# One more Strassen round of the first MoE layer in each of the last two chunks, with part of the side work on GpSimd

## The chip, the cores and the metric

The kernel runs on one core of one Trainium2 chip. The metric is the device time of one execution in microseconds (us); the median of the runs shown is compared.

## The reference

The reference is an attention with "beacon" keys, followed by a two-layer MLP with a leaky ReLU. All inputs are float32; the kernel works in bf16 with float32 sums.

```python
B, H, S, Nb, D = 8, 8, 576, 16, 64            # q, k, v; Nb beacon keys and values
k_all = concat([beacon_k, k]); v_all = concat([beacon_v, v])
scores = q @ k_all.T / sqrt(D)                 # causal for the S keys, the beacons are always seen
x = softmax(scores) @ v_all                    # -> x: 4608 tokens by 512 (H * D)
h = x @ w_in                                   # 4608 x 2048, the first layer
out = maximum(0.01 * h, h) @ w_out             # 4608 x 512, the second layer
```

## The kernel before, in words

**Attention.** The work goes by 32 pairs of heads (8 batches of 4 pairs, index `g`). TensorE makes scores, ScalarE takes the exponential, GpSimd (POOL in the profile) zeroes the causal triangles with a select (L285), TensorE multiplies with the values (`value`, L355), VectorE (DVE) divides by the sums (`rec` L384, then `x_nat` L385), and the result is turned into `xT`, which lies with features on the partitions. The last pair, 31, is turned by TensorE (L401) and copied by VectorE (L406).

**MLP.** The 4608 tokens are cut into nine chunks of 512. The first layer of a chunk has 16 feature blocks of 128. A plain block (`up`, which calls `moe1`) is four matmuls of 512 columns into one PSUM bank (L438) and one Prelu on ScalarE into `gT` (L446). The second layer is done by Strassen's identity in all chunks: `down` makes one half of one of seven products, eight matmuls of 256 columns (L514), 14 downs a chunk. It needs sums of blocks of `gT` (`token_sums`, four VectorE additions for each half of a chunk, recorded at L789), and its products are put together by `combine` (L542, L545) and stored by SyncE (L606).

**Rounds.** In the last two chunks (`TAIL` is 7, so chunks 7 and 8) some blocks of the first layer are also done by Strassen's identity. One round (`in_round`) makes four feature blocks, `2r`, `2r+1`, `8+2r` and `8+2r+1`, with seven products of four 256-column matmuls (L667) in place of 16 matmuls of 512 columns. The products go through five PSUM tiles, in the order 1 and 2 (`one`), 6 (`six`), 5 (`five`), 4 (`four`), 7 (`seven`), 3 (into `five`). ScalarE copies two of them into temporaries (L701, L713), VectorE makes five additions (u2 L710, u3 L721, c21 L722, c12 L724, c22 L725), and ScalarE takes four Prelus (`leave`, L684). The three figures after `R` in the written order say how many downs of the chunk before are put behind product 1, behind product 5 and at the end. A round needs differences of blocks of `w_in`, made once by VectorE for the columns of three rounds (`w_in_sums`, into the idle buffers of the attention; the one for product 7 is written over `w_in_sb[1]`), and sums of blocks of `xT` (`x_in_sums`).

**Order.** All engine queues follow the order of the program. Up to pair 31 a planner spreads ups and downs between the attention's steps: events with a due time in units of pairs are sorted, and `fill` puts ups and downs between them. Small VectorE additions wait in the list `due`; each `up` and each `down` issues one of them (`add_due`). When the attention is over, chunk 6 has all its 14 downs left and chunks 7 and 8 have everything left; this tail is written out by hand, with `u` an up, `d` a down, `R` a round, `x` the sums of `xT`, `t` the first half of a chunk's `token_sums`, and `w` a rest of the weight differences:

```python
last_chunks("D X31 x7 d a1 R111 x8 R111 t u d u d u d u u d u d u u w")
last_chunks("R111 R111 R111 t u d u d u d u d d d14")
```

So chunk 7 has two rounds and eight plain blocks, chunk 8 three rounds and four plain blocks. PSUM tiles for ups, rounds, values and transposes come from a pool of four banks (`ps_one`); in the tail the downs have two buffers of their own (`ps_sc`).

Of the kernel before, what the change touches and what calls it, by code (L numbers as in the profile page):

```python
# [15 lines left out]
def kernel(  # L16
# [606 lines left out]
    def w_in_sums(n, lo=0, hi=ROUNDS, first=False):  # L623
# [7 lines left out]
            (TAIL - 1, dict(out=w_t[n][:, j, cols], in0=x[:, j], in1=y[:, j], op=SUB)) for j in range(2)  # L631
        ]

    def x_parts(i):
# [20 lines left out]
    def in_product(i, n, r, bank, first):  # L655
        (a11, a12), (_, a22) = x_parts(i)
        x = {1: a11, 2: a12, 4: a22}.get(n)
        x = x_sums[i][n] if x is None else x
# [16 lines left out]

    leaves = []

# [13 lines left out]
    def in_round(i, r, downs):  # L691
# [32 lines left out]
        add(out=temps["c12"], in0=five, in1=temps["u2"], op=ADD)  # L724
        add(out=temps["c22"], in0=temps["u3"], in1=temps["p5"], op=ADD)  # L725
        leaves.extend(((i, 2 * r, 1, temps["c21"]), (i, HF + 2 * r, 0, temps["c12"]), (i, HF + 2 * r, 1, temps["c22"])))
# [4 lines left out]
    def last_chunks(steps):  # L731
        for step in steps.split():
            op, n = step[0], int(step[1:] or 1)
            i = done1[0] // NF
            if op == "d":
                for _ in range(n):
# [5 lines left out]
            elif op == "R":  # L742
                in_round(i, done1[0] % NF // 4, [int(x) for x in step[1:]])
            elif op == "X":
                x_transposes(n, nc.vector.tensor_copy)
            elif op == "w":
                w_in_sums(7, ROUNDS - 1, ROUNDS)
            elif op == "x":
# [9 lines left out]
            elif op == "D":  # L758
                later = due[:]
                assert len(later) == 4, len(later)  # L760
                due.clear()
                down()
                down()
                due.extend(later)
            elif op == "t":
                leave_all()
                due.extend((i, op) for op in token_sums(i, 0, SLICE))

# [22 lines left out]

    def add_all(i):
        while due and due[0][0] == i:
            add_due()

# [3 lines left out]
    def up():  # L799
        i1, n = divmod(done1[0], NF)  # L800
        assert i1 < ready[0]
        add_late()
        fc = n if i1 == 0 else n // 2 + n % 2 * HF
        moe1(i1, fc)
        if (i1, n) == (TAIL - 1, 4 * (ROUNDS - 1) + 2):
            w_in_sums(7, 0, ROUNDS - 1, first=True)
            add_due()
        add_due()
        done1[0] += 1
        turn[0] = 1  # L810
# [5 lines left out]
        if i1 and n % (2 * SLICE) == 2 * SLICE - 1:  # L816
            due.extend((i1, op) for op in token_sums(i1, n // 2 + 1 - SLICE, n // 2 + 1))

    def down():
        add_late()  # L820
        add_due()
# [129 lines left out]
    with order:  # L951
# [103 lines left out]
```

## Time and profile before

| | before |
|---|---|
| median of 3 runs | 323.76 us (323.68 to 329.38) |
| the profiled execution: its own time | 325.42 us |
| its span, first to last instruction | 323.7 us |
| TensorE (PE) busy in the span | 313.8 us, 97% |
| weight loads (PEld) | 224.0 us, 69% |
| ScalarE (ACT) | 205.6 us, 64% |
| GpSimd (POOL) | 186.7 us, 58% |
| VectorE (DVE) | 173.2 us, 54% |
| mean granted TensorE clock | 0.998 |

The page gives busy time by engine, the span in 40 slices, the chain of work that ended last, and the costliest groups of instructions by source line. A row of the timeline has start, duration, engine, line, operation, result from operands, shapes and a count; what stands in brackets is the idle time before it and what ended it. Several instructions of one kind in a row are merged into one row. In the rows of TensorE a group's duration contains a modelled pipeline end of about 0.16 us, so the spacing of the starts is the better measure.

### The profile page before, as it was taken

Reading aid. Unit: us, or ns where it says so; the run is one execution under the profiler, and the core shown is the slowest. Engines: PE = TensorE matmul, PEld = TensorE weight load, DVE = VectorE, ACT = ScalarE, POOL = GpSimd, SP = SyncE. Lnnn points to the kernel's source line nnn. Section 1 sums busy time; section 2 is a strip of 40 time slices with the busy share of each in tenths; the row PEclk is TensorE's granted clock in tenths of the full one; section 3 lists DMA queues with packets and bytes.
Section 4 is the critical chain, followed back from the end, with each engine's and each line's share of the span. In section 5 each row is a group of like instructions: output and inputs, shape, how many; then the busy total and the mean of one; then the engine's idle time right before and its main releaser. Section 6 shows DMA issues by size and latency. Waiting matters only on the chain.

```text
span 323.7 us, 8808 instructions
## 1 busy us (share of the span) xinstructions
PE 313.8 (97%) x3517; PEld 224.0 (69%) x3542; DVE 173.2 (54%) x351; ACT 205.6 (64%) x349; POOL 186.7 (58%) x354
## 2 busy tenths in 40 slices
PE   8999999899999999999999999999999999999995
PEld 5565567665678557854788888656875688688784
DVE  3464278635275244444543454525464789577954
ACT  4958974288845786478746874687458547455510
POOL 8895886999998787659875977666221000000000
PEclk9999999999999999999999999999999999999999
DMA  8999999999999999999999999999322101200213
GB/s 135 130 192 189 122 213 134 124 187 208 167 133 154 197 176 132 115 183 98 118 192 191 105 125 118 185 147 108 52 78 84 26 0 34 75 25 0 67 65 131
DMA packets 155769, 39.79 MB, mean 123 GB/s; under 512 B 142368, under 2 KB 153504, under 8 KB 155728
## 3 DMA queue, kind: packets, MB, share of 16 engines
q0 software_dynamic: 99824, 18.54, 89.8%
q1 hardware_dynamic: 55632, 20.62, 37.7%
q8 instruction: 27, 0.44, 0.6%
q14 instruction: 14, 0.11, 0.1%
q10 hardware_dynamic: 272, 0.07, 0.1%
HBM read 37.22 MB, written 9.44 MB: 144 GB/s over the span
## 4 chain that ended last, share of the span: by engine, by line
PE 71%; ACT 3%; DVE 1%; issue 1%; ACTq 0%
PE acc L438 24%; PE acc L514 19%; PE sc L514 11%; PE av L355 6%; PE sc L310 5%; PE acc L667 5%; ACT aT L329 2%; ACT aT L325 1%; DVE x_nat L385 0%; ACT gT L446 0%; DVE gsum L789 0%; DVE p L542 0%; DVE rec L384 0%; PE tp L401 0%; ACTq L329 0%
## 5 line engine op out<-in xcount | busy, mean ns | idle before, releaser
L438 PE MATMUL acc<-xT,w_in_sb 128*128 128x512 bf16 (+1 forms) x535 | 116.4, 354 | 1.8 <-DVE x_nat L385 0.4
L446 ACT ACTIVATE gT<-acc 128x512 bf16<-128x512 f32 x124 | 71.0, 625 | 35.2 <-PE acc L438 35.1
L285 POOL TENSOR_SCALAR_AFFINE_SELECT aT<-aT 128x256 bf16<-128x256 bf16 (+2 forms) x160 | 60.9, 411 | 49.4 <-ACT aT L325 29.9
L438 PEld LDWEIGHTS <-w_in_sb 128*128 128x128 bf16 x560 | 51.7, 98 | 43.4 <-issue 2.5
L514 PEld LDWEIGHTS <-gT 128*128 128x128 bf16 x576 | 54.9, 98 | 9.4 <-issue 2.0
L329 ACT ACTIVATE aT<-sc 128x1024 bf16<-128x1024 f32 (+3 forms) x64 | 51.8, 894 | 0.0
L514 PEld LDWEIGHTS <-gsum 128*128 128x128 bf16 x432 | 40.9, 98 | 7.7 <-issue 0.6
L325 ACT ACTIVATE aT<-sc 128x512 bf16<-128x512 f32 (+3 forms) x64 | 29.0, 521 | 24.7 <-PE sc L310 24.2
L384 DVE RECIPROCAL rec<-av 128x6 f32<-128x6 f32 (+1 forms) x64 | 11.9, 186 | 59.3 <-PE av L355 58.8
L355 PEld LDWEIGHTS <-aT 128*128 128x128 bf16 (+1 forms) x960 | 36.5, 98 | 8.9 <-issue 1.5
L355 PE MATMUL av<-v_aug,aT 128*128 128x65 bf16 (+1 forms) x960 | 39.3, 194 | 0.7 <-DMA v_aug<-in_v_dram 0.7
L210 POOL DMA_DIRECT2D v_aug<-in_v_dram x40 | 34.2, 856 | 5.1 <-DMA w_in_sb<-in_moe_w_in_dram 4.5
L167 POOL DMA_DIRECT2D k_nat<-in_k_dram x48 | 34.8, 730 | 2.8 <-DMA w_out_sb<-in_moe_w_out_dram 2.3
L167 POOL DMA_DIRECT2D q_nat<-in_q_dram x48 | 34.8, 729 | 0.5 <-issue 0.3
L514 PE MATMUL acc<-w_out_sb,gT 128*128 128x256 bf16 x288 | 34.6, 273 | 0.4 <-ACT gT L446 0.4
L385 DVE TENSOR_TENSOR x_nat<-av,rec 128x384 bf16<-128x384 f32 (+1 forms) x64 | 31.4, 491 | 2.4 <-DVE rec L384 0.3
L272 ACT ACTIVATE aT<-sc 128x1024 bf16<-128x1024 f32 (+3 forms) x32 | 25.9, 872 | 3.1 <-PE sc L263 3.0
L789 DVE TENSOR_TENSOR gsum<-gT 128x1024 bf16<-128x1024 bf16 x18 | 12.7, 707 | 23.5 <-ACT gT L446 23.5
L310 PE MATMUL sc<-qT,kT 64*128 64x80 bf16 (+22 forms) x384 | 22.2, 250 | 2.1 <-issue 1.2
L514 PE MATMUL acc<-w_sum,gsum 128*128 128x256 bf16 x192 | 24.0, 273 | 0.0
L310 PEld LDWEIGHTS <-kT 64*128 64x128 bf16 x384 | 13.0, 94 | 12.1 <-issue 8.0
L545 ACT COPY p<-acc 128x512 f32<-128x512 f32 x15 | 9.1, 604 | 14.9 <-PE acc L514 14.9
(95 smaller groups left out, 331.4 us busy)
## 6 DMA issues: line engine op xcount, KB each, us to landing
out_dram<-p SPq DMA_DIRECT2D x26, 256.0 KB, 3.6
q_nat<-in_q_dram POOLq DMA_DIRECT2D x48, 72.0 KB, 5.8
k_nat<-in_k_dram POOLq DMA_DIRECT2D x48, 72.0 KB, 5.4
v_aug<-in_v_dram POOLq DMA_DIRECT2D x24, 128.0 KB, 6.5
w_in_sb<-in_moe_w_in_dram POOLq DMA_DIRECT2D x2, 1024.0 KB, 12.9
w_out_sb<-in_moe_w_out_dram POOLq DMA_DIRECT2D x2, 1024.0 KB, 11.3
out_dram<-u SPq DMA_DIRECT2D x8, 256.0 KB, 4.1
gsum<-in_q_dram POOLq DMA_DIRECT2D x8, 144.0 KB, 6.4
```

The lines of the kernel that those rows point to most:

```text
L167: nc.gpsimd.dma_start(out=t[:, :, par], in_=(q, k)[which][b, 2 * hp + par].rearrange("(t p) d -> p t d", p=NR),)
L210: nc.gpsimd.dma_start(out=dst[lo : ROWS[c], c, :, 0:D], in_=v[b, :, OFF[c] : OFF[c] + n].rearrange("h p d -> p h d"),)
L272: nc.scalar.activation(out=aT[:, :, c0 : c0 + w], in_=sc[:, :, 0:w], func=AF.Exp, scale=0.125)
L285: nc.gpsimd.affine_select(out=view, in_=view, compare_op=ALU.is_ge, fill=0.0, base=128 - n if lo == 0 else 0, channel_multiplier=-1, patte ...
L310: nc.tensor.matmul(out=(sc[par] if apart else sc[:, par])[:, at : at + b - a], lhsT=kT[ps_, c * 128 : (c + 1) * 128], rhs=qT[ps_, q0 : q0 ...
L325: nc.scalar.activation(out=probs[g][:, par, lo:hi], in_=sc[par][:, at : at + hi - lo], func=AF.Exp, scale=0.125)
L329: nc.scalar.activation(out=probs[g][:, :, lo:hi], in_=sc[:, :, at : at + hi - lo], func=AF.Exp, scale=0.125)
L355: nc.tensor.matmul(out=avv[:, n, 0 : D + 1], lhsT=aT[0 : ROWS[c], par, a0 : a0 + 128], rhs=va[0 : ROWS[c], c, 2 * hp + par, :], start=(c = ...
L385: nc.vector.tensor_tensor(out=x_nat[:, t0:t1].rearrange("p t e d -> p (t e) d"), in0=avv[:, :, 0:D], in1=rec[:, n0:n1, None].to_broadcast( ...
L438: nc.tensor.matmul(out=acc[:, lo:hi], lhsT=w_in_cols(fc, j), rhs=xT[:, j, x0 : x0 + hi - lo], start=(j == 0), stop=(j == NJ - 1), skip_gro ...
L446: nc.scalar.activation(out=gT[i][:, fc, :], in_=acc, func=AF.Prelu, alpha=0.01)
L514: nc.tensor.matmul(out=acc[:, lo : lo + HD], lhsT=left(i, n, fc, tile), rhs=right(n, fc), start=(lo == 0 and fc == 0), stop=(fc == HF - 1) ...
```

## The change

Chunk 7 now has three rounds and four plain blocks, chunk 8 four rounds and no plain block. This has five parts.

1. The two written orders of the tail are replaced. The number of downs is the same; they stand at other places. `in_round` counts rounds by chunk (`rounds`), and the plain blocks of the last chunks are those behind the rounds' columns (`ROUNDS_OF`).
2. The fourth round needs weight differences for 256 more columns. They are made by GpSimd (`w_in_last`, eight subtractions of 128x256 bf16), into a value buffer that batch 6 has left, as events due at 31.5 to 32.4 pairs. Of GpSimd's work only the selects of the last score block, due at 31.48, are near.
3. The third round's share of the difference for product 7 (two VectorE subtractions of 128x256) is made behind the up 13 of chunk 6, no longer in chunk 8.
4. In every round the addition c22 is made by GpSimd.
5. `token_sums` of the last chunks' second halves are put in `due` at the end of the chunk (the new step `t3` for chunk 8), and `add_all` can issue a chosen few.

```diff
+    flat_v = v_bufs[(B - 2) % 2].rearrange("p c h d -> p (c h d)")
+    w_last = {
+        n: flat_v[:, i * 512 : (i + 1) * 512].rearrange("p (j f) -> p j f", j=2) for i, n in enumerate((5, 6, 4, 7))
+    }
...
+    def w_in_last(n, eng):
+        cols = slice(ROUNDS * 256, (ROUNDS + 1) * 256)
...
+        x, y = {5: (b12, b11), 6: (b22, w_last[5]), 4: (b21, w_last[6]), 7: (b22, b12)}[n]
+        for j in range(2):
+            eng.tensor_tensor(out=w_last[n][:, j], in0=x[:, j], in1=y[:, j], op=SUB)
...
-                    w = w_t[n][:, j, cols]
+                    w = w_t[n][:, j, cols] if r < ROUNDS else w_last[n][:, j, f : f + 255 : 2]
...
-        add(out=temps["c22"], in0=temps["u3"], in1=temps["p5"], op=ADD)
+        nc.gpsimd.tensor_tensor(out=temps["c22"], in0=temps["u3"], in1=temps["p5"], op=ADD)
...
-        fc = n if i1 == 0 else n // 2 + n % 2 * HF
+        if i1 < TAIL:
+            fc = n if i1 == 0 else n // 2 + n % 2 * HF
+        else:
+            plain[i1] = m = plain.get(i1, -1) + 1
+            fc = 2 * ROUNDS_OF[i1 - TAIL] + m // 2 + m % 2 * HF
...
+        if (i1, n) == (TAIL - 1, 4 * ROUNDS + 1):
+            w_in_sums(7, ROUNDS - 1, ROUNDS, first=True)
+            add_due(2)
...
+        for at, n in ((NG - 0.5, 5), (NG - 0.2, 6), (NG + 0.1, 4), (NG + 0.4, 7)):
+            events.append((at, 7, w_in_last, (n, nc.gpsimd)))
...
-        last_chunks("D X31 x7 d a1 R111 x8 R111 t u d u d u d u u d u d u u w")
-        last_chunks("R111 R111 R111 t u d u d u d u d d d14")
+        last_chunks("D X31 x7 d a1 R110 R111 x8 u R311 d t u u u")
+        last_chunks("R100 R112 t d R200 R111 d d d t3 d14")
```

More of the change, by code (lines that the diff above doesn't have):

```diff
@@ L632, in w_in_sums @@
         ]
+    def w_in_last(n, eng):
+        cols = slice(ROUNDS * 256, (ROUNDS + 1) * 256)
+        (b11, b21), (b12, b22) = (
+            [w_in_sb[i][:, at : at + 2, cols] for at in (0, 2)] for i in range(2)
+        )
+        x, y = {5: (b12, b11), 6: (b22, w_last[5]), 4: (b21, w_last[6]), 7: (b22, b12)}[n]
+        for j in range(2):
+            eng.tensor_tensor(out=w_last[n][:, j], in0=x[:, j], in1=y[:, j], op=SUB)
     def x_parts(i):
@@ L657, in in_product @@
         x = {1: a11, 2: a12, 4: a22}.get(n)
-        x = x_sums[i][n] if x is None else x
+        if x is None:
+            x = x_sums[i][n]
+            if any(op["out"] is x for _, op in due):
+                add_all(i, [x_sums[i][m] for m in (5, 6, 3, 7)])
         for f in range(2):
@@ L674, in in_product @@
                 )
-    leaves = []
+    ROUNDS_OF = (3, 4)
+    leaves, plain, rounds = [], {}, {}
     def leave_all(n=3):
@@ L766, in last_chunks @@
                 leave_all()
-                due.extend((i, op) for op in token_sums(i, 0, SLICE))
+                assert rounds[i] >= n
+                due.extend((i, op) for op in token_sums(i, n // 3 * SLICE, (n // 3 + 1) * SLICE))
     done1, done2, at2, ready, turn, first_down, held = [0], [0], [0, 0], [0], [0], [0], [0]
@@ L790, in add_due, with add_all @@
             n -= 1
-    def add_all(i):
-        while due and due[0][0] == i:
-            add_due()
+    def add_all(i, only=None):
+        mine = [x for x in due if x[0] == i and (only is None or any(x[1]["out"] is t for t in only))]
+        due[:] = [x for x in due if all(x is not m for m in mine)]
+        for _, op in mine:
+            nc.vector.tensor_tensor(**op)
     SLICE = 4
@@ L815, in up @@
                 due.extend((0, first_sums[m][k]) for k in (1, 2, 3) for m in (11, 15))
-        if i1 and n % (2 * SLICE) == 2 * SLICE - 1:
+        if i1 and n % (2 * SLICE) == 2 * SLICE - 1 and (i1 < TAIL or n == NF - 1):
             due.extend((i1, op) for op in token_sums(i1, n // 2 + 1 - SLICE, n // 2 + 1))
     def down():
+        assert at2[0] < done1[0] // NF and all(x[0] != at2[0] for x in leaves)
         add_late()
@@ L1022 @@
         apart_from_values[0] = True
-        last_chunks("D X31 x7 d a1 R111 x8 R111 t u d u d u d u u d u d u u w")
-        last_chunks("R111 R111 R111 t u d u d u d u d d d14")
+        last_chunks("D X31 x7 d a1 R110 R111 x8 u R311 d t u u u")
+        last_chunks("R100 R112 t d R200 R111 d d d t3 d14")
+        assert at2[0] == NCH and not (due or late or leaves)
 _INS = ['q', 'k', 'v', 'beacon_k', 'beacon_v', 'moe_w_in', 'moe_w_out']
```

7 lines of the change are left out of this document (4 added, 3 removed).

## The prediction

> **What bounds the kernel now.** I read the page first, then busy time by stretches of the tail, then the chain of waits, then the engines' own timelines around the rounds.
>
> ```profile
> span 323.7 us, 8808 instructions
> PE 313.8 (97%) x3517; PEld 224.0 (69%) x3542; DVE 173.2 (54%) x351; ACT 205.6 (64%) x349; POOL 186.7 (58%) x354
> POOL 8895886999998787659875977666221000000000
> PE 71%; ACT 3%; DVE 1%; issue 1%; ACTq 0%
> ```
>
> TensorE is busy 97% of the span and is most of the chain that ended last; GpSimd has nothing to do in the last quarter. In the stretches below the columns are busy time of PE, PEld, DVE, ACT and POOL.
>
> ```profile
> 247.50:257.40 9.90, 9.79 (x110) 5.65 (x109) 7.66 (x18) 6.05 (x11) 0.06 (x1) 1.00 0.15 32
> 257.40:282.90 25.50, 25.39 (x208) 19.83 (x207) 19.86 (x36) 12.81 (x23) 0.00 (x0) 1.00 0.10 32
> 282.90:306.10 23.20, 23.15 (x197) 19.24 (x197) 17.81 (x30) 13.79 (x25) 0.00 (x0) 1.00 0.11 36
> 306.10:320.20 14.10, 14.10 (x129) 12.35 (x127) 8.97 (x16) 2.51 (x5) 0.00 (x0) 1.00 0.24 82
> ```
>
> The tail begins at 257.4 and falls into chunk 7's first layer (to 282.9), chunk 8's (to 306.1) and chunk 8's 14 downs. TensorE has no gap in it at a granted clock of 1.00, VectorE is busy 78% of the time, ScalarE 50 to 60%. So the time is the sum of the matmuls, and what a round is worth is a difference of matmul prices, as long as the other engines keep up.
>
> **The matmuls removed and added.** The chain, in order of time (start, length, what, count):
>
> ```profile
> 281.34 1.73 PE acc L438 x8
> ...
> 286.58 1.31 PE acc L667 x12
> ...
> 306.19 14.06 PE sc L514 x128
> ```
>
> A 512-column matmul costs 1.73/8 = 0.216 us, a 256-column one 1.31/12 = 0.109 us (14.06/128 = 0.110 in the downs). So four plain blocks are 16 x 0.216 = 3.46 us and a round is 28 x 0.109 = 3.06 us: 0.40 us less. Two rounds are new: **0.81 us** less. The downs keep their number. Nothing else leaves TensorE's path, so this is the most that the change can give, 0.25% of the time.
>
> **Do the other engines keep up with rounds that stand closer?** The old orders had a down at the end of every round; `R110 R111`, `R100 R112` and `R200 R111` have none there. I take chunk 7's second round of before as the pattern: product 7 begins at 269.88.
>
> ```profile
> 269.88 1.04 PE L667 MATMUL acc<-aT,w_in_sb 128*128 128x256 bf16 x8
> 270.52 0.69 DVE L721 TENSOR_TENSOR kT<-acc,kT 128x512 f32<-128x512 f32 x1 [0.18 <-PE acc L667]
> 271.32 0.69 DVE L722 TENSOR_TENSOR aT<-acc,kT 128x512 f32<-128x512 f32 x1
> 271.93 0.68 DVE L724 TENSOR_TENSOR kT<-acc,kT 128x512 f32<-128x512 f32 x1
> 272.52 0.68 DVE L725 TENSOR_TENSOR aT<-kT 128x512 f32<-128x512 f32 x1
> ```
>
> From the start of product 7, u3 ends at +1.33, c21 at +2.13, c12 at +2.73. Four matmuls take 0.437 us. With no down at the end, the next round's product 6 stands behind products 7 and 3, its own product 1, one down and product 2, so it starts at 4 x 0.437 + 0.874 = +2.62; product 5 follows at +3.06 and product 4 at +3.49 or later. In the program of before the pool hands banks out in the order in which they came free: a round's five tiles lay in banks 4, 7, 5, 6, 4 and the next one's in 7, 4, 6, 5, 7. So `six` takes the bank freed by u3 (+1.33), `five` that of c21 (+2.13), `four` that of c12 (+2.73); each is free 0.7 us or more before it is needed. I cost this at 0; the margins are the cover.
>
> VectorE has 4 additions a round in place of 5, in 7 rounds in place of 5: 28 against 25 at a spacing of 0.60 us, so 1.8 us more in a tail of 62.7 us where it is idle over 20%. Its work before the first round is the same, except that two subtractions (part 3) come earlier. ScalarE has six operations a round (about 3.2 us) where four plain blocks had four: 2.4 us more over both rounds, with 40% idle. I cost both at 0. Where a round has no down behind product 5 (`R100`, `R200`), ScalarE's copy of `five` is close to the matmuls that add to it:
>
> ```profile
> 285.11 0.60 PE L667 MATMUL acc<-aT,aT 128*128 128x256 bf16 x4
> 285.80 0.59 ACT L713 COPY kT<-acc 128x512 f32<-128x512 f32 x1 [0.33 <-PE acc L667]
> ```
>
> Counted from product 5's start the copy ends at +1.28; product 3 would start at 3 x 0.437 = +1.31. That is just met; I take 0.03 us for each of the two, **0.05 us**, and at most 0.2 together if a Prelu stands ahead of the copy.
>
> **c22 on GpSimd.** The trace has no two-operand GpSimd addition. From below, a one-operand float32 cast and from above twice its spacing:
>
> ```profile
> L184 POOL CAST bk<-bk_raw 128x384 bf16<-128x384 f32 x1 | 0.5, 499 | 0.3 <-DMA bk_raw<-in_beacon_k_dram 0.3
> 246.52 1.04 POOL L285 TENSOR_SCALAR_AFFINE_SELECT aT<-aT 128x256 bf16<-128x256 bf16 x3 [0.51 <-PE acc L438]
> ```
>
> 0.50 x 512/384 = 0.67 us and 1.33 us; I take 1.1, nearer to the upper end since two operands are read. It starts when u3 ends, +1.4, and ends by +2.7, where VectorE ended it at +3.3. Who waits: the Prelu on c22, the next copy of `five` (p5, no earlier than +3.7) and the next u3, so a GpSimd time up to 2.3 us costs nothing. At the end of the kernel, behind `t3`, c22's Prelu stands behind a copy and two Prelus on ScalarE and ends near +5.2; product 4 of chunk 8's downs reads it from +6.1, and product 6 needs the second `token_sums` at +7.9, which VectorE can have by +6.9. Cost 0.
>
> **The weight differences on GpSimd.** They are first read in the last round, near 300 us, so their own end is no matter. Where they run is: right behind the selects that end at 247.56, into the ten microseconds where VectorE serves the last values. The two engines do hold each other up:
>
> ```profile
> 82.57 0.19 POOL L225 COPY kT<-bkT 128x16 bf16<-128x16 bf16 x1
> ...
> 126.88 0.75 POOL L225 COPY kT<-bkT 128x16 bf16<-128x16 bf16 x1
> 126.90 0.68 DVE L789 TENSOR_TENSOR gsum<-gT,gsum 128x1024 bf16<-128x1024 bf16 x1
> 87.82 2.22 POOL L285 TENSOR_SCALAR_AFFINE_SELECT aT<-aT 128x256 bf16<-128x256 bf16 x5
> 88.80 0.98 DVE L789 TENSOR_TENSOR gsum<-gT 128x1024 bf16<-128x1024 bf16 x1 [4.01 <-ACT gT L446]
> 105.14 0.41 POOL L285 TENSOR_SCALAR_AFFINE_SELECT aT<-aT 128x256 bf16<-128x256 bf16 x1 [0.44 <-ACT aT L325]
> 105.29 0.69 DVE L542 TENSOR_TENSOR p<-acc,p 128x512 f32<-128x512 f32 x1 [0.58 <-PE acc L514]
> ```
>
> A copy of 0.19 us took 0.75 us beside a VectorE addition of two SBUF operands, and ended when that did; such an addition took 0.98 in place of 0.68 beside selects, and went in between two of them. An addition that reads PSUM (105.29) was not slowed. The Trainium skill, "SBUF — State Buffer", section "SBUF: two separate sides", states it as an exclusive lock: a VectorE operation with two SBUF inputs and a GpSimd operation that reads SBUF take turns for whole instructions. The three pairs of rows agree. By that rule c22 lies beside c21 and c12, which read PSUM, and is not in the way.
>
> Now VectorE's queue where the differences would run, and TensorE's row that depends on it:
>
> ```profile
> 248.53 0.55 DVE L789 TENSOR_TENSOR aT<-w_in_sb,aT 128x768 bf16<-128x768 bf16 x1
> ...
> 250.14 0.55 DVE L789 TENSOR_TENSOR aT<-w_in_sb,aT 128x768 bf16<-128x768 bf16 x1
> 250.61 0.68 DVE L789 TENSOR_TENSOR gsum<-gT 128x1024 bf16<-128x1024 bf16 x1
> 251.21 0.75 DVE L789 TENSOR_TENSOR w_in_sb<-w_in_sb 128x512 bf16<-128x512 bf16 x2
> 252.35 0.18 DVE L384 RECIPROCAL rec<-av 128x4 f32<-128x4 f32 x1 [0.39 <-PE av L355]
> 252.57 0.42 DVE L385 TENSOR_TENSOR x_nat<-av,rec 128x256 bf16<-128x256 f32 x1
> 254.25 2.75 PE L438 MATMUL acc<-xT,w_in_sb 128*128 128x512 bf16 x12
> 259.14 0.42 PE L401 MATMUL tp<-ident,x_nat 112*128 112x112 bf16 x5
> ```
>
> The up at 254.25 takes the bank that the `x_nat` at 252.57 frees at 252.99: 1.26 us of cover. Five subtractions or additions of two SBUF operands stand ahead of it on VectorE. If each lets one GpSimd subtraction pass, `x_nat` comes later by the turns, less its 0.39 us of idle time.
>
> A GpSimd subtraction of 128x256 lies between 0.34 us (one-operand select, 1.04/3) and twice that, 0.68; I take 0.58, again nearer to two reads. In turns from 247.6: two pass, the first VectorE subtraction runs 248.76 to 249.22, one more passes, the `x_nat` of 249.67 runs beside another, then four VectorE operations alternate with three, and the fourth ends at 253.84; `rec` and `x_nat` run to 254.48. The up then starts 0.3 us late, and all of TensorE's work behind it. At 0.50 to 0.54 us an operation the same count gives 0 to 0.2 us, at 0.62 it gives 0.6, at 0.68 it gives 1.0. I take **0.3 us**, from 0 to 1.0. The Trainium skill, "GPSIMD Engine Reference", section "Elementwise — side-by-side cycle accounting", gives 4497 ns for a 2048-element addition, which would be an estimate of 0.56 us for 256 elements, with dispatch on top; the sum by it would hold 0.2 to 0.6 us here.
>
> The moved subtractions of part 3 (0.28 us each in chunk 8) come ahead of the last `x_nat` of pair 31; TensorE reads that at 259.14, 0.9 us behind its end at 258.23, so they cost 0 unless the turns above also reach to there. No DMA is added, and GpSimd issues none behind 247.56; SyncE's stores move only with their downs.
>
> **The sum.** -0.81 + 0.05 + 0.3 = -0.46 us. The profiled execution took 325.42 us, of which 323.7 is span; its 1.7 us outside are left as they are, so it would read 324.96. The median of the runs shown, 323.76, is that much lower than the profiled one and within 0.1 of the span; from it I get **323.3 us**.
>
> **The rivals.**
>
> 1. *GpSimd and VectorE do not get in each other's way at that place* (VectorE's close run of four operations keeps the turn, as the 0.75 us copy may have seen, or GpSimd's subtraction is short). Then only the matmuls count: 323.76 - 0.81 = 322.95.
> 2. *Slower: the turns cost more than the rounds give.* Place: VectorE's queue from 248.5 to 259. The price is the lateness of `x_nat` beyond its 1.26 us, and later of pair 31's last `x_nat` beyond 0.9 us. From 0.65 us a subtraction on it eats the 0.81. At 0.70 us, 1.1 us at 254.25 and up to 0.4 at the last values: 323.76 - 0.81 + 1.5 = 324.45. For it: twice the select is 0.68, and a semaphore between dependent subtractions would lengthen it. Against it: while VectorE works from PSUM or waits, a subtraction passes for nothing.
> 3. *The closer rounds wait for a bank after all*, if `six` (or, behind an up, `one`) should fall on the bank of `five`, which is free at +2.73 where it is wanted at +2.62. What such a wait adds:
>
> ```profile
> 78.81 0.56 DVE L385 TENSOR_TENSOR x_nat<-av,rec 128x384 bf16<-128x384 f32 x1
> 79.42 3.63 PE L438 MATMUL acc<-xT,w_in_sb 128*128 128x512 bf16 x15 [0.41 <-DVE x_nat L385]
> L438 PEld LDWEIGHTS <-w_in_sb 128*128 128x128 bf16 x560 | 51.7, 98 | 43.4 <-issue 2.5
> ```
>
>    TensorE starts 0.05 us behind VectorE's end, and a weight load of 0.1 us may lie open: with the 0.11 above up to 0.26, say 0.2 us at each of four places, 323.3 + 0.8 = 324.1, no gain at all. Against it stands the order of banks given above.
> 4. *The change does not do what it says*, that is a round is no cheaper than four plain blocks when ScalarE or VectorE set its pace: 323.8. The gapless rows of rounds at 1.31 us for 12 speak against it.
>
> **How the numbers follow.** Forecast (0 to 0.6 us lost to the turns) 0.40; rival 1 0.27; rival 2 0.17; rival 3 0.11; rival 4 0.05. The range goes from rival 1 less the 0.2 us or so by which medians differ, 322.7, to rival 2, 324.5. A change of 2% would be 6.5 us, about what a measurement of this kernel can tell from none; every case above is within 1 us or so. So within 2% has 0.97, and 0.01 and 0.02 are left for what I haven't seen (slower for a stall of VectorE's whole queue).
>
> **What the profile after would show.** Right: 196 matmuls in line L667's place against 140 and 32 fewer in the plain blocks' line; no gap of TensorE between the rounds; eight GpSimd subtractions from 247.6 on, each near 0.6 us; VectorE's additions of 248 to 254 stretched; a gap of some tenths at the up behind 254; the last matmul at about 319.8 in place of 320.24. Wrong: gaps of TensorE in front of product 6 or product 3; a GpSimd c22 of over 2.3 us; a TensorE gap over 0.8 us before 260; or VectorE's `x_nat` rows on time, by which the turns were no cost.

## The result, and the profile after

The changed kernel takes 328.06 us (median of 22 runs, 325.52 to 330.83), the kernel before 324.94 us beside it (median of 22, 323.29 to 329.38). The ratio is 1.0081, with a 95% interval of 1.006 to 1.0102: **slower, by about 2.6 us** (2.0 to 3.3). The medians are of all executions, the ratio of those within 1.5% of the fastest of their kernel. I had forecast 323.3 us and a range up to 324.5, from a median of 323.76 for the kernel before; over 22 executions that kernel is at 324.94. The profiled execution took 328.79 us, of which 327.1 is span; the 1.7 us outside the span are as in the profiled execution before.

The page of the changed kernel first: busy time by engine, then GpSimd and the granted TensorE clock in 40 slices.

```profile
span 327.1 us, 8922 instructions
...
PE 316.1 (97%) x3566; PEld 226.8 (69%) x3566; DVE 180.0 (55%) x354; ACT 207.5 (63%) x353; POOL 200.4 (61%) x369
...
POOL 8795887999998787659875977663227003111300
PEclk9999999999999999999999999999999799999999
```

TensorE's busy time rose by 2.3 us although it has less to do, and one slice, from 253.5 us on, has a granted clock below 0.8. The same stretches as before, with a closer look into that slice (columns as there):

```profile
247.50:257.40 9.90, 7.91 (x72) 3.94 (x71) 9.00 (x13) 4.22 (x8) 5.40 (x10) 0.87 0.08 17
254.80:256.00 1.20, 1.20 (x5) 0.44 (x3) 1.17 (x5) 0.00 (x0) 0.00 (x0) 0.50 0.00 0
256.00:257.00 1.00, 1.00 (x4) 0.29 (x2) 1.00 (x3) 0.53 (x1) 0.00 (x0) 0.50 0.00 0
257.00:258.20 1.20, 1.20 (x8) 0.55 (x7) 0.51 (x1) 0.09 (x2) 0.00 (x0) 0.51 0.39 82
257.40:282.90 25.50, 25.50 (x239) 21.09 (x238) 18.61 (x38) 13.05 (x23) 2.55 (x2) 0.98 0.09 28
282.90:306.10 23.20, 23.20 (x203) 19.57 (x201) 20.54 (x32) 15.21 (x28) 5.11 (x4) 1.00 0.11 36
```

In the ten microseconds ahead of the tail TensorE is busy 7.91 us where it was 9.79, and its granted clock is 0.50 to 0.51 from 254.8 to 258.2, 3.4 us. Behind that it has no gap. The three timelines of that place show why; TensorE:

```profile
247.54 0.72 PE L355 MATMUL av<-v_aug,aT 128*128 128x65 bf16 x18
...
254.08 0.73 PE L355 MATMUL av<-v_aug,aT 128*128 128x65 bf16 x18 [1.99 <-DVE x_nat L385]
254.64 3.50 PE L438 MATMUL acc<-xT,w_in_sb 128*128 128x512 bf16 x8
...
321.73 1.91 PE L514 MATMUL sc<-w_out_sb,gsum 128*128 128x256 bf16 x16
```

VectorE and GpSimd:

```profile
248.52 0.42 DVE L385 TENSOR_TENSOR x_nat<-av,rec 128x256 bf16<-128x256 f32 x1
248.86 4.46 DVE L808 TENSOR_TENSOR aT<-w_in_sb,aT 128x768 bf16<-128x768 bf16 x1
...
253.46 0.56 DVE L385 TENSOR_TENSOR x_nat<-av,rec 128x384 bf16<-128x384 f32 x1
```

```profile
246.84 1.04 POOL L285 TENSOR_SCALAR_AFFINE_SELECT aT<-aT 128x256 bf16<-128x256 bf16 x3 [0.51 <-PE acc L438]
247.85 1.29 POOL L645 TENSOR_TENSOR v_aug<-w_in_sb,w_in_sb 128x256 bf16<-128x256 bf16 x2
249.11 2.54 POOL L645 TENSOR_TENSOR v_aug<-w_in_sb,v_aug 128x256 bf16<-128x256 bf16 x4
251.62 1.28 POOL L645 TENSOR_TENSOR v_aug<-w_in_sb 128x256 bf16<-128x256 bf16 x2
```

GpSimd makes its eight subtractions in one piece, 0.635 us each, from 247.85 to 252.90. VectorE's subtraction of two SBUF operands (the row of 0.55 us at 248.53 before, now L808) starts at 248.86, is counted busy for 4.46 us and ends at 253.32, 0.4 us after the last of the eight. An operation that reads PSUM isn't slowed beside them: the `x_nat` at 248.52 takes its 0.42 us. `x_nat` of pair 30's first half follows at 253.46; the second half's values wait for the PSUM bank that it frees, and TensorE has a gap of 1.99 us. Behind the gap eight plain matmuls take 3.50 us; at a granted clock of 1.00 they take 1.89 (the same row of the kernel without the subtractions).

**A length to measure by.** The first 245 us differ by up to some microseconds from execution to execution of one kernel, so I compare from the start of the 18 value matmuls ahead of this place (247.54 above) to the start of the last 16 matmuls (321.73): 74.19 us. Before:

```profile
247.22 0.72 PE L355 MATMUL av<-v_aug,aT 128*128 128x65 bf16 x18
...
318.32 1.91 PE L514 MATMUL sc<-w_out_sb,gsum 128*128 128x256 bf16 x16
```

That is 71.10, so the tail of the profiled execution became 3.09 us longer. The experiments take these apart into **-0.77 (rounds), +2.16 (TensorE waits), +1.70 (lowered clock)**. The third part isn't in every execution (below).

### The profile page after: what moved, and what is told of

Read it like the earlier page. It is cut to its first block, busy times and chain, and to the rows that moved or that the text cites. A ratio compares the mean times of both kernels' runs of the same rounds, so it can differ in the third digit from the quotient of the medians.

```text
span 327.1 us, 8922 instructions
## 1 busy us (share of the span) xinstructions
PE 316.1 (97%) x3566; PEld 226.8 (69%) x3566; DVE 180.0 (55%) x354; ACT 207.5 (63%) x353; POOL 200.4 (61%) x369
## 4 chain that ended last, share of the span: by engine, by line
PE 66%; DMA 2%; POOL 2%; ACT 2%; issue 2%; DVE 1%; POOLq 0%; ACTq 0%
PE acc L438 22%; PE acc L514 16%; PE sc L514 11%; PE acc L683 7%; PE av L355 6%; PE sc L310 5%; DMA v_aug<-in_v_dram 2%; ACT aT L329 1%; POOL aT L285 0%; DVE x_nat L385 0%; POOL k_nat L167 0%; POOL q_nat L167 0%; POOL v_aug L210 0%; ACT aT L325 0%; ACT gT L446 0%
## 5 line engine op out<-in xcount | busy, mean ns | idle before, releaser
L438 PE MATMUL acc<-xT,w_in_sb 128*128 128x512 bf16 (+1 forms) x528 | 111.2, 357 | 0.5 <-DVE x_nat L385 0.5
L446 ACT ACTIVATE gT<-acc 128x512 bf16<-128x512 f32 x116 | 66.3, 627 | 33.8 <-PE acc L438 33.8
L438 PEld LDWEIGHTS <-w_in_sb 128*128 128x128 bf16 x528 | 48.8, 98 | 42.1 <-issue 4.3
L742 POOL TENSOR_TENSOR aT<-kT 128x512 f32<-128x512 f32 x7 | 8.9, 1277 | 48.2 <-DVE kT L738 31.2
L808 DVE TENSOR_TENSOR gsum<-gT 128x1024 bf16<-128x1024 bf16 x18 | 12.4, 691 | 22.0 <-ACT gT L446 21.8
```

The source lines that it names most:

```text
L438: nc.tensor.matmul(out=acc[:, lo:hi], lhsT=w_in_cols(fc, j), rhs=xT[:, j, x0 : x0 + hi - lo], start=(j == 0), stop=(j == NJ - 1), skip_gro ...
L446: nc.scalar.activation(out=gT[i][:, fc, :], in_=acc, func=AF.Prelu, alpha=0.01)
```

## The experiments

**Theory 1**: GpSimd's run of eight keeps the SBUF port that it shares with VectorE until its end, VectorE's subtraction stands still, and TensorE waits for it; the rounds gain what was forecast. ("Port" stands for whatever the two engines share there: the traces show the waiting, not the port.) **Rivals**: the closer rounds cost the time; or the subtractions take turns and something else stops VectorE.

### Without the subtractions, and the subtractions alone

The changed kernel without the eight (it leaves out the fourth round's weight differences, and that round reads what lies in the value buffer):

```diff
-        for at, n in ((NG - 0.5, 5), (NG - 0.2, 6), (NG + 0.1, 4), (NG + 0.4, 7)):
-            events.append((at, 7, w_in_last, (n, nc.gpsimd)))
```

> The changed kernel without the eight GpSimd subtractions (the fourth round's weight differences are left out, so that round multiplies with old values). Theory A (the eight subtractions, run back to back, hold VectorE's two-operand subtraction for their whole 5 us; TensorE then waits 2.0 us for x_nat and loses 1.6 us more while its clock is down): no gap before 262, VectorE's subtraction at 249 back at 0.55 us, clock 1.00, the last matmul 0.75 us earlier than in the kernel before counted from the same start, time about 323.0 to 324.2, some 0.7 us below the kernel before of the same runs and 3 to 4 us below the changed kernel. Theory B (the closer rounds or the GpSimd c22 cost the time, and the gap is incidental): stays 2 us or more above the kernel before.

Measured 324.25 us against 325.33, ratio 0.995 (0.9925 to 0.9975). No gap, clock 1.00, VectorE's subtraction 0.55 us, length 70.33: 0.77 less than before. The counterpart is the kernel before with `w_last`, `w_in_last` and those two lines, and nothing else of the change.

> The kernel before with only the eight GpSimd subtractions added; nothing reads them. Theory A: the whole loss and more, a gap of about 2 us of TensorE near 252 to 254, in many executions a clock at half speed for about 3 us behind it; 3 to 4 us above the kernel before. Theory B: within 0.5 us of the kernel before.

Ratio 1.0116 (1.0051 to 1.0182), from six executions that lie far apart: 326.35 and 326.62, and four from 331.43 to 332.81. The rows are from the first, VectorE's, then TensorE's:

```profile
246.95 4.46 DVE L802 TENSOR_TENSOR aT<-w_in_sb,aT 128x768 bf16<-128x768 bf16 x1
```

```profile
252.18 0.73 PE L355 MATMUL av<-v_aug,aT 128*128 128x65 bf16 x18 [2.00 <-DVE x_nat L385]
252.74 1.89 PE L438 MATMUL acc<-xT,w_in_sb 128*128 128x512 bf16 x7
```

The same 4.46 us and the same gap, with no round added. The length is 73.26, 2.16 more than before; here the clock behind the gap stayed full (1.89 us). So the loss in the length hangs on the eight subtractions, and a gap of 2.0 us costs the clock in some executions only. The four executions near 332 are 5 us longer still; no trace shows where.

How often the clock falls is known only by its mean over an execution: 0.995 or less in 9 of 22 executions of the changed kernel, 2 of these 6, 1 of 12 without the subtractions, and 8 of the 70 of the kernel before that ran beside the experiments. Such a mean doesn't say where the clock was low: in one kernel below (memsets between the subtractions) it is 0.983, and that clock was 0.50 from 10 to 16 us and 1.00 behind the gap. If all nine lost their clock here, the three parts come to -0.77 + 2.16 + 9/22 x 1.70 = 2.1 us, an estimate, beside the 2.6 measured (2.0 to 3.3).

### The same subtractions on VectorE

```diff
-        for at, n in ((NG - 0.5, 5), (NG - 0.2, 6), (NG + 0.1, 4), (NG + 0.4, 7)):
-            events.append((at, 7, w_in_last, (n, nc.gpsimd)))
+        for n in (5, 6, 4, 7):
+            events.append((NG - 0.5, 7, w_in_last, (n, nc.vector)))
```

> The changed kernel with the eight subtractions on VectorE, all due at 31.5, in its idle stretch of 4.3 us between 243.7 and 248 (8 x 0.28 us = 2.2 us). Theory A: no wait of TensorE, 0.7 us below the kernel before, as without the subtractions: about 0.998 of its time. Theory B, or if VectorE is short of time there: at or above the kernel before.

Ratio 0.9975 (0.9946 to 1.0005), length 70.34, no gap. In VectorE's idle stretch ahead of the values all eight take 1.7 us. The interval reaches 1, so the length is what shows the gain. With c22 on VectorE too, so that GpSimd does nothing of the change:

```diff
-        nc.gpsimd.tensor_tensor(out=temps["c22"], in0=temps["u3"], in1=temps["p5"], op=ADD)
+        add(out=temps["c22"], in0=temps["u3"], in1=temps["p5"], op=ADD)
```

> As the run with the subtractions on VectorE, and c22 back on VectorE too, so GpSimd does nothing of the change. If GpSimd's c22 is free but not needed: the stretch from the values at 247 to the last matmul within 0.2 us of that run, time the same. If VectorE needs the relief (7 x 0.60 = 4.2 us more in the tail, where chunk 7's rounds follow each other without a down): gaps of TensorE of 0.1 to 0.6 us ahead of products 6 and 5 in the first rounds, together up to 1.5 us.

Ratio 0.9963 (0.9929 to 0.9997), length 70.33. c22 on GpSimd was free and brought nothing.

### The gap filled

Ten matmuls on zeros, into a free PSUM tile, ahead of the values that wait.

```diff
+            if what is value and args == (NG - 2, 1):
+                idle = ps_sc.tile([128, 2, 512], FP32, name="sc", tag="sc")
+                for _ in range(10):
+                    nc.tensor.matmul(
...
```

> The changed kernel with ten matmuls of 512 columns of zeros (2.2 us, results unused) put ahead of the values on which TensorE waits. If the half clock behind the gap comes from TensorE being idle for 2 us: the clock stays at 1.00, the eight matmuls behind take 1.73 us in place of 3.34, and the time falls by about 1.4 us against the changed kernel in the executions that lost the clock, to about 1.5 us above the kernel before or less. If the clock drop has another cause (or zeros do not count as work), the eight matmuls still take 3.3 us.

```profile
251.16 2.32 PE L1054 MATMUL sc<-blank 128*128 128x512 bf16 x10
253.32 0.73 PE L355 MATMUL av<-v_aug,aT 128*128 128x65 bf16 x18
253.89 1.89 PE L438 MATMUL acc<-xT,w_in_sb 128*128 128x512 bf16 x7
```

(The last row is a group of eight with one record missing, as above.) Ratio 1.0018 (0.9989 to 1.0047), length 72.51: the wait is still there (2.18 over the kernel without subtractions), the slow matmuls behind it are gone, and none of 12 runs shows a clock below 0.998. 74.19 - 72.51 = 1.68 us is the price of the clock in the profiled execution. The Trainium skill, "TensorE: Matmul & The Clock Gate", section "HAM oscillation — how this bites in real kernels", warns of idle gaps over about 3.4 us. Here 1.99 us was enough in the profiled execution of the changed kernel. It wasn't in three others: gaps of 2.00 us (the subtractions alone), 2.18 and 2.25 us (two kernels below) left the clock at 1.00. The rows behind the one of 2.18:

```profile
257.59 0.73 PE L355 MATMUL av<-v_aug,aT 128*128 128x65 bf16 x18 [2.18 <-DVE x_nat L385]
258.15 1.89 PE L438 MATMUL acc<-xT,w_in_sb 128*128 128x512 bf16 x8
```

### What the run holds

From here on each kernel ran once, except the two whose ratio is given. These single executions lie between 322.12 and 330.62 us, since the first 245 us differ, so what is read is the duration of an operation and the length, not the time. In place of the subtractions eight GpSimd copies, then the subtractions with a memset of two columns behind each (the copies leave the fourth round's differences out):

```diff
-            eng.tensor_tensor(out=w_last[n][:, j], in0=x[:, j], in1=y[:, j], op=SUB)
+            eng.tensor_copy(out=w_last[n][:, j], in_=x[:, j])
```

> The changed kernel with the eight GpSimd subtractions replaced by eight GpSimd copies of the first operand (the fourth round's differences are so left out). One read in place of two, the same place, the same eight in a row. I expect 0.35 us each, 2.8 us in all. If any unbroken GpSimd run that reads SBUF holds the port: VectorE's subtraction at 249 takes about 1.9 to 2.2 us, until the last copy. If operations with one read give way, as the selects did (0.98 in place of 0.68): at most 0.9 us, and no gap of TensorE.

> The changed kernel with a GpSimd memset of 128x2 (0.1 us, reads nothing) behind each of the eight subtractions. If an instruction that does not read sets the port free: VectorE's subtraction gets in behind one GpSimd subtraction, 1.3 us or less, the later ones take turns with it, and TensorE's gap falls under 0.6 us. If the run holds the port all the same: VectorE's subtraction takes 4.5 us or more and the gap is 2 us or more.

The copies (GpSimd, then VectorE):

```profile
246.76 2.79 POOL L645 COPY v_aug<-w_in_sb 128x256 bf16<-128x256 bf16 x8
```

```profile
247.78 2.17 DVE L808 TENSOR_TENSOR aT<-w_in_sb,aT 128x768 bf16<-128x768 bf16 x1
```

The copies end at 249.55, VectorE's operation 0.4 us later: held to the end of a shorter run, within the cover, so TensorE had no gap (323.89 us). With the memsets it was held for 4.72 us (gap 2.25, 327.72 us): 0.06 us without an SBUF read between two subtractions doesn't let VectorE in. Eight one-operand selects, which leave out the same differences:

> The changed kernel with eight one-operand selects of 128x256 on GpSimd in place of its eight subtractions (the weight differences of the last round are left out). Theory 1 (any unbroken GpSimd run that reads SBUF keeps the port to its end): eight selects take about 2.8 us, from 246.8 or so to 249.6, and VectorE's two-operand subtraction that meets them is held until the last ends, 1.5 to 2.5 us, as beside the eight copies. Rival (selects give way, as in the kernel before at 88.80): that operation takes 0.9 us or less, and ends while selects are still to come. TensorE has no gap in either case.

Held too, 2.30 us beside 2.91 us of selects (324.31 us). So among these three kinds the kind of GpSimd operation doesn't matter. One rival stays open: in every kernel that was held, the operation held is the same subtraction, and it reads `w_in_sb`, as GpSimd's eight do. No run held another one, so these runs don't exclude that the common tile plays a part.

### When they do take turns

Each pair of subtractions made to wait for a ScalarE copy of one column, which was done before GpSimd came to it:

```diff
+        nc.scalar.copy(out=w_last[n][:, :, 0:1], in_=x[:, :, 0:1])
         for j in range(2):
             eng.tensor_tensor(out=w_last[n][:, j], in0=x[:, j], in1=y[:, j], op=SUB)
```

> The changed kernel with the eight GpSimd subtractions cut into four pairs: ahead of each pair ScalarE writes one column of its result (a copy of 128x2 values that the pair writes over), so that a pair waits for ScalarE's place in the order. Theory A (a run of GpSimd subtractions holds the port until it pauses): VectorE's subtraction near 249 waits for one pair at most, 1.3 us, and takes no more than 1.9 us in place of 4.46; TensorE's gap of 2.0 us is gone or under 0.3 us, and from the values at 247 to the last matmul it is as short as without the subtractions; about 0.7 us under the kernel before. Theory C (VectorE gets the port back only when all GpSimd work is done, or loses as much time as GpSimd works): the gap stays near 2 us.

GpSimd's first three pairs, the ScalarE copies of the second and third, and two of VectorE's operations:

```profile
246.30 1.29 POOL L646 TENSOR_TENSOR v_aug<-w_in_sb,w_in_sb 128x256 bf16<-128x256 bf16 x2
247.56 3.62 POOL L646 TENSOR_TENSOR v_aug<-w_in_sb,v_aug 128x256 bf16<-128x256 bf16 x4
247.07 0.36 ACT L644 COPY v_aug<-w_in_sb 128x2 bf16<-128x2 bf16 x2
247.31 0.71 DVE L809 TENSOR_TENSOR aT<-w_in_sb,aT 128x768 bf16<-128x768 bf16 x1
...
249.51 1.15 DVE L809 TENSOR_TENSOR gsum<-gT 128x1024 bf16<-128x1024 bf16 x1
```

Ratio 0.996 (0.9927 to 0.9992), length 70.33, no gap. GpSimd still works without a pause from 246.30 to 252.81, and VectorE gets in: 0.71, 0.67, 1.15 and 2 x 0.85 us. That is the turn-taking of my forecast, in a run that begins at the same place: 0.31 us behind the first values, with VectorE's subtraction 1.01 us behind the start of the run, both as in the changed kernel. The addition at 249.51 reads `gT`, not `w_in_sb`, and takes turns like the others. In the next three only the first of the eight waits, for a small VectorE memset on the buffer that it writes over:

```diff
+        def mark(n):
+            nc.vector.memset(w_last[n][:, :, 0:1], 0.0)
+
+        events.append((NG - 0.37, 3, mark, (5,)))
+        for n in (5, 6, 4, 7):
+            events.append((NG - 0.37, 3, w_in_last, (n, nc.gpsimd)))
```

> The changed kernel, with the first of GpSimd's eight subtractions made to wait for a small VectorE memset that stands right behind VectorE's x_nat near 248.6 us; from there VectorE has its two-operand subtraction ready, and may hold the port when the eight begin. Theory 1 (an unbroken GpSimd run keeps the port to its end, whoever had it before): at most the first two-operand VectorE operation runs in 0.55 us, the next one is held 3.5 to 5 us, and TensorE has a gap of 1.5 us or more before 258. Rival (turns are taken once VectorE held the port when the run began): no VectorE operation over 1.2 us, the GpSimd subtractions stretched to about 1 us each, TensorE's gap 0.6 us or less.

> The kernel of the run before last once more (GpSimd's eight subtractions begin behind a VectorE memset, while VectorE's two-operand subtraction holds the port), now for its time. If the order in which the two engines come to the port is the whole loss, it gives back all of it: from the first values to the last downs 70.3 us as in the run without the subtractions, no gap of TensorE, 0.7 to 0.8 us less than the kernel before, a ratio of 0.995 to 0.999, and no execution below a granted clock of 0.997 more often than the kernel before. Rival (part of the loss stays, as an extra wait or a lowered clock that a single look missed): a ratio of 1.000 or more.

```profile
245.49 0.55 DVE L808 TENSOR_TENSOR aT<-w_in_sb,aT 128x768 bf16<-128x768 bf16 x1
...
246.86 0.76 DVE L808 TENSOR_TENSOR aT<-w_in_sb,aT 128x768 bf16<-128x768 bf16 x1
247.54 1.15 DVE L808 TENSOR_TENSOR gsum<-gT 128x1024 bf16<-128x1024 bf16 x1
248.62 1.70 DVE L808 TENSOR_TENSOR w_in_sb<-w_in_sb 128x512 bf16<-128x512 bf16 x2
250.24 0.17 DVE L384 RECIPROCAL rec<-av 128x4 f32<-128x4 f32 x1
250.44 0.42 DVE L385 TENSOR_TENSOR x_nat<-av,rec 128x256 bf16<-128x256 f32 x1
```

```profile
245.67 1.53 POOL L645 TENSOR_TENSOR v_aug<-w_in_sb,w_in_sb 128x256 bf16<-128x256 bf16 x2 [1.17 <-DVE v_aug L1032]
247.16 3.68 POOL L645 TENSOR_TENSOR v_aug<-w_in_sb,v_aug 128x256 bf16<-128x256 bf16 x4
250.81 2.26 POOL L645 TENSOR_TENSOR v_aug<-w_in_sb 128x256 bf16<-128x256 bf16 x2
```

The rows are VectorE's, then GpSimd's, of the timed kernel; its first execution (323.68 us) had the same durations. 323.23 us against 325.77, **ratio 0.9932 (0.9899 to 0.9964)**, length 70.34, no gap: the change with one memset more is faster than the kernel before. The ratio is 2.2 us, below the 0.995 to 0.999 that I had expected, and the length explains 0.76 of it. Part of the rest lies outside the span, 2.6 to 3.7 us in 5 of the 17 executions of the kernel before and at most 1.8 in these 12; the other part isn't explained. The eight take 7.4 us in place of 5.1, since now they wait for VectorE. I took this for proof that whoever holds the port when the run begins decides. It isn't: with the memset one instruction earlier, ahead of `x_nat`, the run begins while the port is free.

> The same kernel with VectorE's memset one instruction earlier, ahead of the x_nat near 247.3 us in place of right behind it, so that GpSimd's eight subtractions begin some 0.2 to 0.3 us sooner, while VectorE works from PSUM and the port is free. Theory 1 (what decides is who holds the port when the run begins): VectorE's two-operand subtraction is held to the end of the run, 4 to 5 us, TensorE gets a gap of 1.5 to 2.5 us, and the stretch from the first values to the last downs is 72.2 us or longer. Rival (a semaphore wait at the head of the run, or its later place, is what opened it to turns): no VectorE operation over 1.2 us, no gap, 70.3 us.

```profile
246.01 0.81 DVE L810 TENSOR_TENSOR aT<-w_in_sb,aT 128x768 bf16<-128x768 bf16 x1
```

GpSimd had begun at 245.74, and VectorE still got in behind its first subtraction (length 70.34): that theory fell. Two kernels then moved one thing each: VectorE's request (`x_nat` done three times over), and the run (20 GpSimd memsets of two columns ahead of it, no wait and no pause).

> The kernel with the memset ahead of x_nat, and VectorE's x_nat of that half done three times over (the same result; it reads PSUM), so that its two-operand subtraction asks for the port about 1.1 us after GpSimd's run has begun, as in the changed kernel (1.0 us), in place of 0.3 us. Theory A (VectorE gets its turns only where it meets the run within its first instruction or so; who comes later finds it closed): that subtraction is held to the end of the run, 3.5 to 5 us. Theory B (the pause of 0.7 us, or the wait, ahead of the run is what leaves it open): no two-operand VectorE operation over 1.2 us, and no gap of TensorE over 0.6 us.

> The changed kernel with 20 GpSimd memsets of two columns (about 0.06 us each) between the selects and its eight subtractions: no wait and no pause stand ahead of them, but they begin some 1.2 us later, about when VectorE's two-operand subtraction starts. Theory A (meeting the run at its first instruction decides): VectorE gets turns, no two-operand operation over 1.2 us, no gap of TensorE over 0.6 us. Theory B (only a pause or a wait ahead of the run leaves it open): the operation that meets the run is held to its end, 3.5 to 5 us, the first one or the next; TensorE's gap is 1.5 us or more.

In the first VectorE asked 1.18 us after the start of the run, 0.07 us ahead of a seam between two subtractions, and ran in 0.55 us. In the second the memsets took 0.66 us in all, VectorE asked 0.4 us after the start and got its turns (0.67, 0.63, 1.15, 2 x 0.85; length 70.34). So no wait is needed, and neither theory was decided. Both places inside the second subtraction:

> The kernel with the memset ahead of x_nat once more (GpSimd's eight behind a pause and a wait), with rec and x_nat of that half done twice over, so that VectorE's two-operand subtraction asks for the port about 0.95 us after the run has begun: in the middle of GpSimd's second subtraction, as in the changed kernel, and not at the seam between two as in the kernel with three x_nat. Theory A (VectorE gets its turns only where it asks within the run's first instruction, or just at a seam): held to the end of the run, 4 to 4.7 us; TensorE's gap 1.5 us or more. Theory B (the pause ahead of the run leaves it open): no two-operand VectorE operation over 1.2 us, no gap.

> The kernel with memsets between the selects and GpSimd's eight, 6 of them in place of 20 (0.03 us each by that run, so the eight begin 0.2 us later than in the changed kernel and VectorE asks about 0.85 us after their start, within the second subtraction; with 20 it asked 0.4 us after, within the first). No pause and no wait in either. Theory A: held to the end of the run, 4 us or more, TensorE's gap 1.8 us or more, from the first values to the last downs 72.2 us or longer, where 20 memsets gave 70.3. Rival (memsets of any number ahead of the run open it): no two-operand operation over 1.2 us, 70.3 us.

The first, behind a wait and a pause, with a request 0.94 us after the start:

```profile
249.25 0.77 DVE L818 TENSOR_TENSOR aT<-w_in_sb,aT 128x768 bf16<-128x768 bf16 x1
```

The second, with six memsets (0.2 us) ahead, no wait and no pause, and a request 0.82 us after the start:

```profile
252.19 4.64 DVE L810 TENSOR_TENSOR aT<-w_in_sb,aT 128x768 bf16<-128x768 bf16 x1
```

One takes turns, the other is held to the end (gap 2.18 us, length 72.68). Last, whether it is the time for which GpSimd has had the port to itself, with a wait and a pause ahead and later requests (more repeats of `rec` and `x_nat`):

> The kernel with the memset ahead of x_nat (pause of 0.7 us and a wait ahead of GpSimd's eight), with rec and x_nat of that half repeated three times more, so that VectorE asks for the port about 2.3 us after the run has begun; TensorE waits for that anyway, so its gap is not the measure. Theory C (what decides is how long GpSimd has had the port to itself when VectorE asks: up to 1.25 us it was let in at the next seam, at 2.0 us or more it was held): the two-operand subtraction is held to the end of the run, 2.5 to 3.5 us. Theory B (the pause ahead of the run leaves it open, however late the request): 1.2 us or less.

> The same with two repeats, so that VectorE asks about 1.65 us after the run has begun, between the 1.25 us at which it was let in and the 2.0 us at which it was held. Theory C: either, which narrows the bound: 1.2 us or less, or 3 to 4 us. Theory B: 1.2 us or less.

Turns in both (0.67 and 0.72 us for the operation that meets the run, which asks 2.29 and 1.62 us after the start). That theory falls as well. In the four kernels that repeat `x_nat` TensorE waits 0.36 to 1.06 us at the up behind the next values; that comes with VectorE's added work.

**What is settled and what is open.** Held to the end of the run: the changed kernel, the subtractions alone, copies, selects, memsets between, six memsets ahead. In all of them the eight follow the three selects within 0.3 us and none of the eight waits for another engine. Turns: every kernel in which an instruction of the run waits for another engine, be the wait already met (the ScalarE copies, no pause) or just met (the VectorE memset, 0.7 to 1.2 us of pause), and the one with 0.66 us of memsets ahead of the run. Which property of the queue makes the difference these runs don't tell; a wait and 0.66 us of work without an SBUF read both opened it, and I have no single rule for the two.

## Why the prediction was wrong

**The step that failed** is the term "in turns from 247.6", 0.3 us from 0 to 1.0. It had the right place and the right two engines, and assumed that each VectorE operation waits for one GpSimd instruction at most. I had read that from the row at 88.80, a select run in which VectorE did get in; eight selects in a row, in the experiment, held it to their end. Here it waited for all that was left of the run: 4.46 - 0.55 = 3.9 us in one piece. The upper end, 1.0, came from the same count with a longer instruction, so the range could not hold it either. The Trainium skill, "SBUF — State Buffer", section "Who interferes with whom", says that the first to start has the port for the whole instruction and that the order of issue decides who blocks. The kernels with turns agree: no VectorE operation waited there for more than one subtraction, 0.635 us. The held ones differ on the size: the loser was blocked for the rest of one instruction and six more. And the order alone didn't decide between the two: in seven kernels the run was first by 0.27 to 2.29 us, and VectorE still got its turns.

**The bank.** I gave the cover of the up at 254.25 (1.26 us). The stall came one bank earlier, at the values of pair 30's second half. Their bank was freed in the kernel before at 250.23 and used at 251.60, 1.37 us of cover; from the first anchor `x_nat` now ends 3.47 us later, and TensorE starts 2.16 us later there. For turns alone my bank was the right one: in the timed kernel with the VectorE memset its `x_nat` ends at 250.86, 6.70 us behind the anchor where it was 5.77, and 0.93 of the 1.26 us of cover are used up; with the ScalarE copies, where the run begins at the forecast's place, it is 1.07. So turns cost 0 and not 0.3.

**The clock** was in no term. I costed a gap at its length; this one cost 1.7 us more in the profiled execution.

**The base.** Of the 4.8 us between my 323.3 and the measured 328.06, 1.2 are the kernel before, which I took from three executions. From 324.94 the same sum gives 324.5, with a range up to 325.7, and the measured time lies outside that too.

**Rival 2** (slower, VectorE's queue from 248.5 on) was right in sign and place, but not in mechanism. Its price, 1.5 us of stall at 0.70 us a subtraction, came by turns too; the measured one was 2.16 with 0.635 us a subtraction, and the clock on top. At 0.635 it had itself put the loss below the 0.81 of the rounds, so its sign came out by luck.

**What held.** The rounds: -0.81 + 0.05 = -0.76 forecast, -0.77 measured (70.33 against 71.10), at their full price only once nothing stood in front of them. There are 196 matmuls in the rounds' line and no gap between rounds; the closer rounds' banks cost nothing. The chain shows the two places without a down behind product 5 (start, length, what, count). Each group is the six products of the round behind product 1 and the product 1 of the next round; 28 x 0.109 is 3.05 to 3.06 us:

```profile
288.15 3.09 PE acc L683 x28
...
300.41 3.07 PE acc L683 x28
```

So the copy of `five` cost 0.03 and 0.01 at most, where I took 0.03 each. c22 on GpSimd was sized at 1.1 us, 0.67 to 1.33, and takes 1.28; nobody waits for it, and VectorE's additions from PSUM beside it keep their 0.69:

```profile
L742 POOL TENSOR_TENSOR aT<-kT 128x512 f32<-128x512 f32 x7 | 8.9, 1277 | 48.2 <-DVE kT L738 31.2 <-issue 17.0
```

The subtraction was sized at 0.58 us (0.34 to 0.68) and takes 0.635. Of what I had named as a sign of being wrong, "a TensorE gap over 0.8 us before 260" is what the profile shows. The change stayed within 2%, which I had given 0.97.

## What to carry to other kernels

Work put on an idle engine is free only if it shares nothing with the engine on the path: before moving a run of GpSimd operations beside VectorE operations of two SBUF operands, cost the whole run as one block, not an instruction, and look whose PSUM bank waits behind it. Here the same eight operations cost nothing when VectorE made them in a stretch where it was idle, or on GpSimd when an instruction of the run waited for another engine. And a TensorE gap of 2 us may cost nearly twice its length, by the clock behind it: 1.99 us cost 1.7 more in one of the four traces with such a gap.

## What the hardware did that I had not expected

- A run of eight GpSimd instructions, not one, held up a VectorE subtraction of two SBUF operands: 4.46 us for what takes 0.55 (eight subtractions), 2.17 (copies), 2.30 (selects). A two-column memset between them did not let it in, 4.72.
- Waits of GpSimd for ScalarE copies that were already done let VectorE in (its operations 0.67 to 1.15 us, GpSimd's run stretched from 5.1 to 6.5 us).
- Behind a TensorE gap of 1.99 us the granted clock was 0.50 to 0.51 for 3.4 us (3.50 us for eight matmuls that take 1.89 otherwise); behind gaps of 2.00, 2.18 and 2.25 us in three other traces it stayed at 1.00. With the gap filled by matmuls on zeros, none of 12 executions has a mean clock below 0.998, where 9 of 22 have 0.995 or less with it.
- A float32 addition of 128x512 takes 1.28 us on GpSimd and 0.68 on VectorE.
